# Two clears of unused rows, moved among the block loads of a batch, in a fused Fourier mixing and SwiGLU kernel

## The chip, the cores and the metric

The kernel runs on one core of a Trainium2 chip. The metric is the device time of one execution in microseconds; lower is better. The core's engines run side by side, each with its own instructions in a fixed order: TensorE (PE in the profile, PEld for its weight loads), VectorE (DVE), ScalarE (ACT), GpSimd (POOL) and SyncE (SP), which here only issues DMAs. Engines wait for each other, and for DMAs, by semaphores. The DMAs of SP stand in one queue (q1 in the profile) and are carried by 16 DMA engines.

## The reference

```
X = np.fft.fft(x, axis=1)            # x: 8 batches, 3008 rows, 256 columns
X = np.fft.fft(X, axis=2)
x = X.real.reshape(24064, 256)
g = x @ w_gate                       # 256 -> 1536
silu = g * (1.0 / (1.0 + np.exp(-g)))
val = x @ w_val
out = (silu * val) @ w_out           # 1536 -> 256
```

## The kernel before

The real part of a two-dimensional Fourier transform has symmetries, and the kernel folds the input by them before it multiplies: rows that differ by a quarter, a half or a reflection of the batch are added and subtracted first, so that the products with the cosine and sine tables are a fraction of the full ones. The transform along the columns is folded into the weights (Wp, Wq, Wm). Each column of the folded problem yields two output rows, a "plus" and a "minus" one.

**Stages.** Batch 0 is loaded and transformed by a prologue written out by hand. All the rest is a stream of units: 24 tiles of up to 512 columns, 12 slices of the hidden width each. A unit does its gate and value products (L1105 on PE), its activations (ACT), its products of gate and value (DVE, or POOL at L1213 and L1256), and the output products (L1283 on PE) follow one tile later. Between the units the later batches are loaded (SP), folded (POOL, the lines L214 to L238) and transformed (L1414 on PE).

**What sets the order.** A planner (class Sched) is given every operation with an estimated time, its dependencies and a due time, chooses the order on each engine, and then issues all operations in that order. So each engine's order is fixed when the program is built. The planner decides by its own estimates, not by what an operation really issues: an operation that issues two DMAs is one entry to it.

**A batch's input.** It goes into two buffers, XA and XC (128 rows of 16 x 256 floats each). XA takes the 128 fold positions from one side, XC the other 60 positions. A batch uses 64 of XC's 128 rows: the second batch (b = 1) rows 64 to 127, a later even batch rows 0 to 63. Each half has 60 rows of data and 4 unused ones, 60 to 63 and 124 to 127. `load_c` returns the steps that fill one half:

- 15 rising blocks (L197), each 4 rows by 4 x 512 floats, 32 KB
- 4 falls (L199), each 60 rows by 512 floats, 120 KB
- a single row (L201), 4 x 256 floats, 4 KB: the batch's first row, which goes into row 124 (60 for even batches), the first of the four unused rows

The unused rows take part in the fold and the products and must hold zeros. `clear_rest` (L326) writes them with one DMA a half, 4 rows by 16 x 256 floats, 64 KB, from a row of zeros kept in Af, a scratch buffer of the fold that POOL clears at L611. The clears are needed once: no later load but the single row writes these rows. The single row lies in a row that a clear writes, so it must come behind the clear of its half.

`load_a` fills XA in the same way: 16 rising blocks of 8 rows (L188, 64 KB each) and 4 falls of 128 rows (L190, 256 KB each). For the second batch XA's rising blocks overwrite space in which the raw weights lay, and its falls space in which the angles of the odd tables lay.

**SP's order around the change.** It is: the loads of batch 0; the 15 rising blocks of XC, the 4 falls, the two clears and the single row; 14 rising blocks of XA; L1569, which copies the first row of a tile's Qt to 16 rows (br); the last two rising blocks; L1577, which spreads br to 128 rows (bc) and waits for br to land; the 4 falls of XA; and then the next loads, the stores of finished output (L1295) and so on. SP's DMAs use eight completion semaphores in turn, and each DMA waits for the one that used its semaphore before, which was issued eight places earlier.

**What the loads feed.** The fold of XC on POOL (L214 to L238, two halves q = 0 and 1, ten instructions each) reads all rising blocks and falls of XC and the clear of its half; the single row is read by the second half alone. Then POOL folds XA in the same ten steps (on 128 rows). Among these steps stand POOL's products of gate and value, L1256, each of which reads a pair of slices from one of two buffers, sv0q and sv1q. ScalarE (L1225) and VectorE (L1249) write the next pair into the same buffer when L1256 has read it.

In the unit loop, the diff touches the place where the steps of the second batch's XC are put on the list of loads:

```
        if i == 1:
            steps = load_c(1, nc.sync)
            pad_row = steps.pop()
            steps.append(lambda: [clear_rest(...) for h in range(2)] + [pad_row()])
            loads.extend((("C", 1), k, fn) for k, fn in enumerate(steps))
```

Of the kernel before, what the change touches and what calls it, by code (L numbers as in the profile page):

```python
# [71 lines left out]
def kernel(  # L72
# [33 lines left out]
    NCR = GH - P  # L106

    def width(t):
        return wide[t]
# [76 lines left out]
    def load_a(b, q):  # L186
        X3 = XA.rearrange("p a q d -> p a (q d)")
        return ([lambda h=h: q.dma_start(out=X3[LA * h:LA * (h + 1), 0:4, :],  # L188
                                         in_=up_block(b, JA - LA * h, LA)) for h in range(NA)] +
                [lambda a=a: q.dma_start(out=X3[:, 4 + a, :], in_=down_set(b, a, JA, LA, NA)) for a in range(4)])  # L190

    def load_c(b, q):

        X3 = XC.rearrange("p a q d -> p a (q d)")
        p0 = 64 * (b % 2)
        pm = p0 + NCR
        return ([lambda h=h: q.dma_start(out=X3[p0 + LC * h:p0 + LC * (h + 1), 0:4, :],  # L197
                                         in_=up_block(b, JC - LC * h, LC)) for h in range(NC_)] +
                [lambda a=a: q.dma_start(out=X3[p0:p0 + NCR, 4 + a, :], in_=down_set(b, a, JC, LC, NC_))  # L199
                 for a in range(4)] +  # L200
                [lambda: q.dma_start(out=XC[pm:pm + 1, 0:4, 1],  # L201
                                     in_=rows_at(b, 0, [[R * D, 1], [R * D, 4], [1, D]]))])
# [121 lines left out]
    def clear_rest(hi, zeros, r0):  # L324
        n = zeros.shape[0]
        nc.sync.dma_start(out=X3c[64 * hi + NCR + r0:64 * hi + NCR + r0 + n, :].rearrange("p (c d) -> p c d", d=D),  # L326
                    in_=zeros.unsqueeze(1).to_broadcast([n, 16, D]))
# [282 lines left out]
    zeros = Af.rearrange("p a b d -> p (a b d)")[:, 0:D]  # L610
# [16 lines left out]
    def pq_tiles(t):  # L627
        if t not in ptile:
            w = width(t) + B if t == nT - 1 else T
            ptile[t] = (pqp if t < nT - 1 else const).tile([P, w], BF16, name="Pt")  # L630
            qtile[t] = (pqp if t < nT - 1 else const).tile([P, w], BF16, name="Qt")
        return ptile[t], qtile[t]
# [155 lines left out]
    def rows(r0, n, step):  # L788
        return out[r0:r0 + step * (n - 1) + 1:step, :]
# [297 lines left out]
    def pe_us(n):  # L1087
        return (n + 6) / 2400

    def act_us(n, ptr=0, sbuf=0):  # L1090
        return n / 1200 + (0.088 if sbuf else 0.0605) + 0.1245 * ptr
# [17 lines left out]
    def bank(k):  # L1109
        return PS[:, (0, 7, 6, 3, 2, 5, 1, 4)[S.place[k[0]]], :]  # L1110
# [20 lines left out]
    def turn(unit, step):  # L1131
        S.turn = (*unit.u, step == "b")
        getattr(unit, step)()
        S.turn = None
# [207 lines left out]
    def run_loads(n):  # L1342
        for what, k, fn in loads[:n]:
            up = NA if what[0] == "A" else NC_
            k_ = k if what[0] == "A" else k % (NC_ + 5)
            S.add("SP", 0.35 if k_ < up else 0.62 if what[0] == "A" else 0.9, fn, w=[((what[0],), k)], lat=LOAD_LAT,
                  ring=RING.get(what, RING[what[0]])[k_ >= up],
                  after=[(("A",), "pre" if k >= NA else "preW")] if what == ("A", 1) else ())
        del loads[:n]
# [222 lines left out]
    def all_rows(t):  # L1572
        w = row_width(t)

        def fn():
            bc[t] = bcp.tile([P, T], BF16, name="bc")
            nc.sync.dma_start(out=bc[t][:, :w], in_=T_["br", t][0:P:8, :w].unsqueeze(1).to_broadcast([16, 8, w]))  # L1577
        return fn
# [13 lines left out]
    for i, u in enumerate(units):  # L1592
        t, f = u
        for op in before.pop(i, ()):
            op()
        if i == 1:
            steps = load_c(1, nc.sync)
            pad_row = steps.pop()
            steps.append(lambda: [clear_rest(1 - h, zeros[64 * (1 - h) + NCR:64 * (1 - h) + 64], 0) for h in range(2)] + [pad_row()])
            loads.extend((("C", 1), k, fn) for k, fn in enumerate(steps))  # L1600
        if i == 8:
            loads[0:0] = [(("A", 1), k, fn) for k, fn in enumerate(load_a(1, nc.sync))]
        run_loads(LOADS)
        if i == FIRST - 1:
            kb = (("B", "bc", 3), 0)

            def first_copy():
                bc[3] = bcp.tile([P, T], BF16, name="bc")
                nc.scalar.copy(bc[3][:, :width(3)], bank(kb)[:, :width(3)])

            S.add("PE", pe_us(T), lambda: nc.tensor.matmul(bank(kb)[:, :width(3)], sel, pq_tiles(3)[1][:, :width(3)], start=True, stop=True),
                  r=[(("pq", 3), "Q")], w=[kb], new=[kb[0]], cat="pe", bits=(0, width(3)))
            S.add("ACT", act_us(T), first_copy, r=[kb], w=[(("bc", 3), 0)], new=[("bc", 3)])
        for j, k in enumerate((i - ROW_GAP, i)[::-1]):
            tr, fr = divmod(k, nF)
            if k >= 0 and fr == {0: 11, 1: 3, 2: 99}.get(tr, 6) and tr + 1 < nT:
                if j:
                    S.add("SP", 0.55, all_rows(tr + 1), r=[(("br", tr + 1), 0)], w=[(("bc", tr + 1), 0)], new=[("bc", tr + 1)], lat=5.0, ring=0.4)
                else:
                    S.add("SP", 0.55, first_rows16(tr + 1), r=[(("pq", tr + 1), "Q")], w=[(("br", tr + 1), 0)], new=[("br", tr + 1)], lat=4.0, ring=0.2)  # L1620
        if i == 2 * nF + 1:
            S.add("ACT", 1.36, lambda: nc.scalar.activation(Wm[:, 1], Wm[:, 1], AF.Copy, scale=-0.5),
                  r=[(("Wm",), (fc, 1)) for fc in range(1, 3)], w=[(("Wm",), 1)])
        if i == nF + 1:
            S.add("DVE", 0.5, lambda: vts(Wg[:, 0], Wm[:, 0], scalar1=-0.5, scalar2=None, op0=Alu.mult),
                  r=[(("Wm",), (fc, 0)) for fc in range(1, 3)], w=[(("Wg",), 0)])
        turn(U[i], "a")
        if owork:
            owork.run(4)
        if i + 1 < len(units):  # L1630
            turn(U[i + 1], "seed")
        if prev is not None:
            turn(U[i - 1], "b")
            if prev[1] == nF - 1:
                owork = OWork(prev[0])
            if owork:
                owork.run(4)
        for what, j in fold_at.get(i, ()):
            fold_step(what, j, i)
        for what in act_at.pop(i, ()):  # L1640
            load_next(what)
        if i in spread_at:
            spread_op(spread_at[i])
        if i in job_at:
            transform_op(*job_at[i])
        prev = u
# [36 lines left out]
```

## Time and profile before

| | |
|---|---|
| median of 3 runs | 606.92 us (605.4 to 607.07) |
| the profiled execution | 604.51 us |
| its span, from the first to the last instruction | 602.7 us |
| granted TensorE clock, mean | 1.00 |
| PE busy | 594.7 us, 99% of the span |
| ACT, DVE, POOL busy | 567.2, 561.3, 547.0 us |
| read from HBM, written to it | 29.43 MB, 24.65 MB |

The profile is a page on one execution and a trace that can be asked for more. Views used below:

- the stretches: busy time of each engine in a window of time, in the order PE, PEld, DVE, ACT, POOL, each with its count of instructions in brackets, then the granted clock, the mean busy share of the 16 DMA engines and the GB/s that they moved
- the timeline: start and duration in us, engine, line, operation, what it writes and reads, shapes, count, and in square brackets the idle time of the engine before it with what ended it; instructions of a kind that follow each other are one row, and SPq is SP's issuing of DMAs, not their transport
- the waits: who waited for whom, in us in total, how often, and the longest
- the list of DMA issues: target and source, count, KB each and, where it is known, us from issue to landing

Idle time of an engine that is not the bottleneck costs nothing by itself.

### The profile page before, as it was taken

What the parts mean: (1) busy time and instruction counts of PE and PEld (TensorE: products, weight loads), DVE (VectorE), ACT (ScalarE), POOL (GpSimd) and SP (SyncE); (2) the same over time, 40 slices, a digit from 0 to 9 for tenths busy, and PEclk for the clock granted to TensorE, in tenths of its full rate; (3) what the DMA queues carried; (4) which work ended last, traced back from release to release, by engine and by line L of the source; (5) the groups of instructions that cost most, each with busy time, mean ns of one, the idle gap of its engine ahead of it and who ended that gap; (6) DMA issues with size and microseconds to landing.
All of it is one profiled execution on the core that took longest, in us unless ns stands there. A gap on an engine that the chain in (4) does not pass through costs nothing.

```text
span 602.7 us, 12697 instructions
## 1 busy us (share of the span) xinstructions
PE 594.7 (99%) x4050; PEld 393.1 (65%) x4050; DVE 561.3 (93%) x1044; ACT 567.2 (94%) x1100; POOL 547.0 (91%) x508
## 2 busy tenths in 40 slices
PE   8999989999999999999999999999999999999997
PEld 6545657666666766666666666666666666666686
DVE  8768989989889999999999999999999999999994
ACT  7899889999998999999999999999999899999995
POOL 7978899999999999999998999998989889868873
PEclk9999999999999999999999999999999999999999
DMA  9835437445504514454223412236121211212112
GB/s 242 134 85 127 135 110 188 122 116 133 145 21 112 152 55 130 119 137 129 62 68 96 111 45 63 72 82 174 47 62 36 66 44 46 61 47 68 53 54 79
DMA packets 49968, 57.70 MB, mean 96 GB/s; under 512 B 7256, under 2 KB 36956, under 8 KB 49902
## 3 DMA queue, kind: packets, MB, share of 16 engines
q1 hardware_dynamic: 46947, 53.64, 33.2%
q0 software_dynamic: 2448, 2.36, 2.6%
q10 hardware_dynamic: 507, 0.91, 0.6%
q8 instruction: 31, 0.51, 0.3%
q14 instruction: 35, 0.29, 0.2%
HBM read 29.43 MB, written 24.65 MB: 90 GB/s over the span
## 4 chain that ended last, share of the span: by engine, by line
PE 90%; ACT 4%; POOL 2%; DMA 1%; issue 1%; DVE 1%; POOLq 0%; ACTq 0%; DVEq 0%
PE ps L1105 44%; PE ps L1283 40%; PE ps L1414 4%; DMA XA<-in_x_dram 1%; PE ps L654 1%; POOL hm L1256 1%; DVE SA L503 0%; PE ps L494 0%; PE ps L545 0%; ACT Tab L429 0%; PE ps L528 0%; ACT wk5s L1225 0%; ACT Tab L1552 0%; ACT SDf L423 0%; ACT wk0s L1193 0%
## 5 line engine op out<-in xcount | busy, mean ns | idle before, releaser
L1105 PE MATMUL ps<-Pt,Wp 128*128 128x512 bf16 (+2 forms) x576 | 203.1, 375 | 0.9 <-ACT sv0q L1225 0.3
L1283 PE MATMUL ps<-Wo,hm 128*128 128x256 bf16 (+2 forms) x1140 | 164.3, 273 | 0.0
L1283 PE MATMUL ps<-Wo,hp 128*128 128x256 bf16 (+2 forms) x1140 | 162.7, 272 | 0.0
L1105 PE MATMUL ps<-Qt,Wq 128*128 128x512 bf16 (+2 forms) x440 | 159.9, 375 | 0.0
L1283 PEld LDWEIGHTS <-hm 128*128 128x128 bf16 (+2 forms) x1140 | 111.8, 98 | 58.1 <-issue 1.1
L1283 PEld LDWEIGHTS <-hp 128*128 128x128 bf16 (+2 forms) x1140 | 112.0, 98 | 53.0 <-issue 0.3
L1256 POOL TENSOR_TENSOR hm<-sv0q 128x1024 bf16<-128x1024 f32 (+2 forms) x68 | 126.7, 1864 | 9.9 <-ACT sv0q L1225 5.6
L1256 POOL TENSOR_TENSOR hm<-sv1q 128x1024 bf16<-128x1024 f32 (+2 forms) x66 | 122.9, 1863 | 9.0 <-DVE sv1q L1249 3.9
L1105 PE MATMUL ps<-Qt,Wm 128*128 128x512 bf16 (+2 forms) x286 | 102.1, 376 | 2.2 <-ACT wk2s L1193 1.6
L1168 ACT ACTIVATE ps<-bc,w 128x512 f32<-128x512 bf16 (+2 forms) x136 | 95.7, 718 | 0.5
L1105 PEld LDWEIGHTS <-Wp 128*128 128x128 bf16 x576 | 56.2, 98 | 31.1 <-issue 3.5
L1225 ACT ACTIVATE sv0q<-ps 128x512 f32<-128x512 f32 (+1 forms) x87 | 57.5, 672 | 3.0 <-PE ps L1105 1.4
L1105 PEld LDWEIGHTS <-Wq 128*128 128x128 bf16 x440 | 43.0, 98 | 26.5 <-issue 2.4
L1225 ACT ACTIVATE sv1q<-ps 128x512 f32<-128x512 f32 (+1 forms) x85 | 55.6, 668 | 3.8 <-POOL hm L1256 3.0
L1105 PEld LDWEIGHTS <-Wm 128*128 128x128 bf16 x286 | 27.9, 98 | 15.7 <-issue 1.3
L214 POOL TENSOR_TENSOR SDf<-XA 128x1020 f32<-128x1020 f32 x14 | 33.0, 2360 | 4.5 <-DMA out_dram<-wk7s 4.5
L224 POOL TENSOR_TENSOR Af<-EOf 128x516 f32<-128x516 f32 (+1 forms) x22 | 24.2, 1102 | 0.4
L221 POOL TENSOR_TENSOR EOf<-SDf 128x512 f32<-128x512 f32 (+1 forms) x22 | 24.0, 1093 | 0.0
L218 POOL TENSOR_TENSOR EOf<-SDf 128x512 f32<-128x512 f32 (+1 forms) x22 | 24.0, 1092 | 0.0
L1178 DVE SCALAR_TENSOR_TENSOR wk10s<-bc,w,ps 128x512 f32<-128x512 bf16 (+2 forms) x32 | 23.2, 726 | 0.2 <-PE ps L1105 0.2
L1105 PE MATMUL ps<-Qt,Wg 128*128 128x512 bf16 (+2 forms) x61 | 22.6, 371 | 0.0
L1414 PE MATMUL ps<-Tab,St 128*128 128x376 bf16 (+1 forms) x64 | 20.0, 323 | 0.0
(447 smaller groups left out, 1411.5 us busy)
## 6 DMA issues: line engine op xcount, KB each, us to landing
XA<-in_x_dram SPq DMA_DIRECT2D x30, 256.0 KB
XA<-in_x_dram SPq DMA_DIRECT2D x112, 64.0 KB
XC<-in_x_dram SPq DMA_DIRECT2D x31, 120.0 KB
XC<-in_x_dram SPq DMA_DIRECT2D x105, 32.0 KB
bc<-br SPq DMA_DIRECT2D x21, 128.0 KB
out_dram<-wk0s SPq DMA_DIRECT2D x19, 128.0 KB
St<-Fc SPq DMA_DIRECT2D x14, 128.5 KB
out_dram<-wk7s SPq DMA_DIRECT2D x13, 128.0 KB
```

Of the source, the lines that this page charges most:

```text
L214: tt(F[:, :, 1:D], up[:, :, 1:D], down[:, :, D - 1:0:-1], op=Alu.add)
L218: tt(E[:, :, 0:P], F[:, :, P:0:-1], F[:, :, P:D], op=Alu.add)
L221: tt(O[:, :, 0:P], F[:, :, P:0:-1], F[:, :, P:D], op=Alu.subtract)
L224: tt(Af[r], EOf[r, :, 0:2, :], EOf[r, :, 2:4, :], op=Alu.add)
L654: nc.tensor.matmul(ps[:, e], Z0[:, q, k, :], Tab[:, c, q, 0, e], start=False, stop=True, skip_group_check=True)
L1105: nc.tensor.matmul(ps[:, :n], Wt[:, gv, fs], src[:, :n], start=start, stop=stop, skip_group_check=True)
L1168: nc.scalar.activation(bank(k)[:, :self.wp], bc[self.t][:, :self.wp], AF.Copy, scale=w0[:, gv, self.f:self.f + 1])
L1178: nc.vector.scalar_tensor_tensor(work(e)[:, :self.wp], bc[self.t][:, :self.wp], w0[:, gv, self.f:self.f + 1], bank(k)[:, :self.wp], op0=Al ...
L1225: return lambda: nc.scalar.activation(self.silu(self.sm, w), src()[:, :w], AF.Silu)
L1256: lambda: nc.gpsimd.tensor_tensor(tiles_of(t)[1][:, f - 1:f + 1, :w], pair(self.vm)[:, :, :w, 1], pair(self.vm)[:, :, :w, 0], op=Alu.mult),
L1283: nc.tensor.matmul(bank(ko)[:n, j * D:(j + 1) * D], hts[t][minus][:, f, c:c + n], Wo[:, f, :], start=(f == 0), stop=(f == nF - 1))
L1414: nc.tensor.matmul(ps[:, cols], l, r_, start=(i == 0), stop=(i == len(mms) - 1), skip_group_check=True)
```

## The change

The two clears are no longer issued in one step with the single row behind the falls. The clear of rows 124 to 127 is issued in the same step as the ninth rising block of XC, right behind it, and the clear of rows 60 to 63 with the tenth. The single row is a step of its own behind the falls. The list of loads is as long as before (20 steps), and the planner's entries keep their times and dependencies, so that its order of entries is the same on every engine.

```
@@ -1596,7 +1596,13 @@
         if i == 1:
             steps = load_c(1, nc.sync)
             pad_row = steps.pop()
-            steps.append(lambda: [clear_rest(1 - h, zeros[64 * (1 - h) + NCR:64 * (1 - h) + 64], 0) for h in range(2)] + [pad_row()])
+            for h in range(2):
+                def clear_too(rows=steps[8 + h], hi=1 - h):
+                    rows()
+                    clear_rest(hi, zeros[64 * hi + NCR:64 * hi + 64], 0)
+
+                steps[8 + h] = clear_too
+            steps.append(pad_row)
             loads.extend((("C", 1), k, fn) for k, fn in enumerate(steps))
```

In SP's queue the second batch's XC then reads: 9 rising blocks, a clear, a rising block, a clear, 5 rising blocks, 4 falls, the single row.

## The prediction

> **What bounds the kernel now.** I read the page first, then the busy time by stretches, then the waits of TensorE, and from the largest one back through the engines that it hangs on. In the rows of part 1 of the page and of the stretches, the figures are busy microseconds.
>
> ```profile
> span 602.7 us, 12697 instructions
> PE 594.7 (99%) x4050; PEld 393.1 (65%) x4050; DVE 561.3 (93%) x1044; ACT 567.2 (94%) x1100; POOL 547.0 (91%) x508
> ...
> 40.00:76.90 36.90, 36.84 (x230) 22.60 (x229) 31.27 (x53) 30.99 (x58) 31.88 (x37) 1.00 0.51 121
> 76.90:81.00 4.10, 2.24 (x13) 1.11 (x12) 3.72 (x6) 3.85 (x8) 4.02 (x4) 1.00 0.33 100
> 81.00:596.00 515.00, 514.96 (x3541) 345.18 (x3540) 495.81 (x899) 496.47 (x972) 478.67 (x401) 1.00 0.33 88
> ```
>
> PE (first figure after the length) is full from 81 us to the end at a granted clock of 1.00, and full from 40 to 76.9. So a microsecond won before 81 us is kept to the end, and the only PE time to be won behind the start lies between 76.9 and 81. It is made of two waits:
>
> ```profile
> 78.58 0.38 PE L1105 MATMUL ps<-Qt,Wm 128*128 128x512 bf16 x1 [1.60 <-ACT wk2s L1193]
> 80.52 0.38 PE L1105 MATMUL ps<-Pt,Wp 128*128 128x512 bf16 x1 [0.27 <-ACT sv0q L1225]
> ...
> 76.93 0.64 ACT L1225 ACTIVATE sv1q<-ps 128x512 f32<-128x512 f32 x1 [1.81 <-POOL hm L1256]
> ...
> 76.93 0.69 DVE L1249 SCALAR_TENSOR_TENSOR sv1q<-wk4s,ps 128x512 f32<-128x512 f32 x1 [1.65 <-POOL hm L1256]
> ```
>
> PE waits for ScalarE, and ScalarE and VectorE both stand until POOL's product L1256 has freed the buffer sv1q. Together 1.60 + 0.27 = 1.87 us, 0.31% of the time: this is the most that the change can bring, since a bound behind POOL would only lower it.
>
> POOL does that product late because its fold of the second batch (L214 and on) stands in front of it, in order:
>
> ```profile
> 62.25 2.35 POOL L214 TENSOR_TENSOR SDf<-XA 128x1020 f32<-128x1020 f32 x1 [4.51 <-DMA out_dram<-wk7s]
> ...
> 64.72 1.90 POOL L1256 TENSOR_TENSOR hm<-sv0q 128x1024 bf16<-128x1024 f32 x1
> ...
> 72.52 2.36 POOL L214 TENSOR_TENSOR SDf<-XA 128x1020 f32<-128x1020 f32 x1
> ...
> 74.98 1.91 POOL L1256 TENSOR_TENSOR hm<-sv1q 128x1024 bf16<-128x1024 f32 x1
> ```
>
> From 62.25 to 76.89 POOL has no gap: no row between them shows one. Before 62.25 it idles 4.51 us. The releaser is named after a store, whose completion counter the loads share; L214 reads XA, and what it needs is the last load of XA. SP's queue shows why that load is late:
>
> ```profile
> 21.70 8.78 SPq L197 DMA_DIRECT2D XC<-in_x_dram  x15
> 30.84 3.53 SPq L199 DMA_DIRECT2D XC<-in_x_dram  x4
> 34.62 2.16 SPq L326 DMA_DIRECT2D XC<-Af  x2
> 40.29 0.65 SPq L201 DMA_DIRECT2D XC<-in_x_dram  x1
> 41.17 7.14 SPq L188 DMA_DIRECT2D XA<-in_x_dram  x14
> 48.86 0.59 SPq L1569 DMA_DIRECT2D br<-Qt  x1
> 49.57 1.02 SPq L188 DMA_DIRECT2D XA<-in_x_dram  x2
> 54.35 0.61 SPq L1577 DMA_DIRECT2D bc<-br  x1
> 55.06 2.51 SPq L190 DMA_DIRECT2D XA<-in_x_dram  x4
> ...
> SPq L201 <- DMA XC<-Af: 3.4, 1, 3.4
> SPq L1577 <- DMA br<-Qt: 3.7, 1, 3.7
> ```
>
> The single row (L201) waits 3.4 us for the clears (L326) to land, and all behind it waits too: the sixteen rises of XA (L188), the row copies L1569 and L1577, the four falls of XA (L190), and then POOL. How the transfers fill the DMA engines meanwhile (the last two figures are the mean share of 16 engines and GB/s):
>
> ```profile
> 33.00:37.00 4.00, 3.81 (x38) 1.74 (x37) 2.55 (x6) 4.00 (x8) 2.64 (x6) 1.00 0.54 125
> 38.50:41.00 2.50, 2.50 (x17) 1.56 (x16) 2.12 (x5) 2.45 (x6) 2.27 (x6) 1.00 0.19 31
> 41.00:42.00 1.00, 1.00 (x7) 0.49 (x5) 1.00 (x2) 1.00 (x2) 1.00 (x1) 1.00 0.03 9
> 42.00:43.00 1.00, 1.00 (x8) 0.58 (x6) 0.49 (x2) 1.00 (x4) 1.00 (x1) 1.00 0.43 125
> 43.00:53.00 10.00, 10.00 (x55) 5.12 (x53) 8.35 (x17) 9.10 (x18) 9.84 (x14) 1.00 0.54 87
> ```
>
> The clears run alone on 0.19 x 16 = 3 engines until 41, then almost nothing moves for 1 us, and from 42 on XA's rises keep 0.54 x 16 = 8.6 engines full for ten microseconds.
>
> **The change part by part.** No instruction of PE, DVE, ACT or POOL is added, taken away or moved. SP issues the same 22 DMAs for XC; the two clears now stand behind the ninth and tenth rise instead of behind the falls. So two clears are passed by the last five rises and the four falls, the tenth rise by one, and the wait of L201 for a clear becomes a wait of the clears' followers for a place in flight: SP keeps eight DMAs in flight, each new one waiting for the one issued eight before (so the built program has it). The clears themselves gain no wait of substance: what they need of POOL (the zeroed rows, and the last reader of the space they overwrite) ends before 23 us, ahead of the ninth rise:
>
> ```profile
> 15.38 0.32 POOL L611 MEMSET Af<- 128x256 f32 x1
> 21.78 1.13 POOL L406 TENSOR_SCALAR XA<-XC,cols 128x376 int32<-128x376 f32 x2
> 26.29 0.25 SPq L197 DMA_DIRECT2D XC<-in_x_dram  x1
> 30.23 0.25 SPq L197 DMA_DIRECT2D XC<-in_x_dram  x1
> ```
>
> *What SP's order gives.* The last two rows are the ninth and the fifteenth rise: 6 steps in 3.94 us, 0.66 us each. Eight in flight make 5.3 us, so the ninth rise lands near 26.3 + 5.3 = 31.6. A clear of 64 KB at the 31 GB/s of its row takes 2.1 us. The clear behind it lands at 33.7, the tenth rise at 34.3, the second clear at 36.5. In the new order the third fall waits for the second clear's place: 36.5. Then the fourth fall, L201 and the first rise of XA follow at 0.88 us each (3.53 / 4 for a fall; 41.17 - 40.29 behind L201): 39.1, against 41.17 now. That is 2.0 us. The upper bound of the clears' cost here: the load of Wo shares these engines until 37.3,
>
> ```profile
> Wo<-in_moe_w_out_dram POOLq DMA_DIRECT2D x1, 768.0 KB, 14.4
> 22.86 0.87 POOL L739 DMA_DIRECT2D Wo<-in_moe_w_out_dram  x1
> ```
>
> and if it halves the rate of the first clear (4.2 us in place of 2.1), the rises of XA begin at 41.2: gain nothing.
>
> *What the engines' work gives.* The clears are not made smaller, and their bytes now lie ahead of the falls' on the same few engines. Those engines were busy to 41.0 (their row), so XA's rises can begin there at about 41.1, if the same work takes the same time, against 42.0 now: 0.9 us, the empty microsecond of the row 41 to 42. The Trainium skill, "DMA: Bandwidth & Descriptors", section "Why a DMA increments its semaphore by 16 and not by 1", has a DMA from this queue run on the largest number of engines up to 16 that divides its slowest dimensions, and on the lowest-numbered ones; 4 rows would be the same four engines for rises and clears, 8 rows eight of them. The 3 and 8.6 engines of the rows agree, and by that rule alone the sum would be 0.9 and not 2.0.
>
> Between 0.9 (same work, same engines) and 2.0 (SP's order alone), with 0 at the slow clear, I take 1.0, nearer to the engines' row, since it needs no guess of how two queues share. The bounds kept are -0.5 and 2.0.
>
> *From there to the end.* The rises of XA run at what the row of 43 to 53 allows, 87 GB/s, whenever they begin; L1569 follows the fourteenth of them and waits for nothing else (its source is written at 45.90, below; it is issued at 48.86), L1577 waits for L1569, and the XA falls stand behind L1577. So the fold moves up by the same 1.0. POOL has room: it is idle from 62.25 - 4.51 = 57.74. The product at 64.72 needs sv0q, complete at 62.30, and that at 74.98 needs sv1q, complete at 72.03, so they can move up 2.4 and 2.9 us:
>
> ```profile
> 45.30 0.60 DVE L1439 TENSOR_TENSOR Qt<-ps,wk0s 128x240 bf16<-128x240 f32 x2
> 61.62 0.68 DVE L1249 SCALAR_TENSOR_TENSOR sv0q<-wk9s,ps 128x512 f32<-128x512 f32 x1
> 71.35 0.68 ACT L1225 ACTIVATE sv1q<-wk3s 128x512 f32<-128x512 f32 x1
> ```
>
> 1.0 us off POOL is then 1.0 us off the wait of 1.60.
>
> *What may be late next.* XC's own falls now land behind the clears, near 41.5 in place of 38.5 (from where the clears run alone), and the fold of XC starts at 40.85, right behind other POOL work. A start at 41.5 would cost 0.7 us of the 4.51 us that POOL idles afterwards, so nothing; were that cover gone, 0.7 us.
>
> ```profile
> 40.03 0.73 POOL L1547 MEMSET Tab<- 64x756 bf16 x1
> 40.85 2.35 POOL L214 TENSOR_TENSOR SDf<-XC 64x1020 f32<-64x1020 f32 x1
> ```
>
> Sum: 1.0 us less. The profiled execution took 604.51 us with a span of 602.7; it would take 603.5. It lies 2.4 us under the median of 606.92, and on that scale the change gives 605.9.
>
> **The rivals.** *The whole wait goes.* If the clears run beside the load of Wo at no cost, SP's order decides: 2.0 us, cut to the 1.87 us of the two waits: 605.1. For it: 13 of 16 engines are idle at 38.5 to 41. Against it: the few that carry the clears are not.
>
> *Nothing moves.* The rises of XA begin when their engines are free, and these finish later because falls and clears now meet there: 606.9. For it: 125 GB/s at 33 to 37 with 8.6 engines shows that falls and rises slow each other already. Against it: the empty microsecond at 41 goes in any case.
>
> *The clears hold up the falls.* Place: the queue of eight. The third fall cannot be issued before the second clear has landed, and the fourth, L201 and all of XA stand behind. The tipping point is a landing of the second clear at 38.5 (2.0 us later than in the sum); slower by 0.3% from 40.3 on, that is when both clears take over 8 us in place of 4.2. For it: a clear took 5.6 us from issue to landing (34.62 to the end of L201's wait, 36.78 + 3.4 = 40.2). With 5.6 for the first and 2.1 for the second XA begins 1.5 us later than now: 608.4. With 5.6 for both it is 5 us: 611.9. Against it: most of those 5.6 us were spent behind falls.
>
> **How the numbers follow.** About 0.3% (1.8 us) is what a measurement of this kernel can tell from no change. Forecast (0.5 to 1.6 us less) 0.42; the whole wait 0.23; nothing 0.17; clears late 0.18. Faster by over 0.3%: 0.19 of the whole wait, whose 1.87 us lie just past the bound, and 0.09 of the forecast by scatter: 0.28. Slower: 0.16 of the late clears and 0.03 by scatter: 0.19. The rest, 0.53, is within. The predicted time is 605.9. The range reaches from the whole wait with some scatter, 604.6, to the milder late clear, 608.2; the forecast's own is 605.3 to 606.4.
>
> **What would show it.** In SP's queue L201 no longer waits for XC<-Af, and the first L188 stands near 40 in place of 41.17 (later than 41.17: the clears hold up the falls). In the stretches the row of 41 to 42 is no longer empty. POOL's first fold of XA starts near 61.2 in place of 62.25, and PE's wait of 1.60 us shrinks by as much. The prediction is wrong if the fold of XA moves and PE's wait does not, if L188 moves and the fold does not, or if PE gains a wait before 76 us.

## The result, and the profile after

| | before | after |
|---|---|---|
| median | 606.93 us (605.4 to 607.53, 6 runs) | 602.9 us (602.02 to 604.11, 6 runs) |
| profiled execution, its span | 604.51 us, 602.7 us | 603.96 us, 602.2 us |

The ratio is 0.9937 with a 95% interval of 0.9919 to 0.9956: faster by 4.0 us, and outside the range of the prediction (604.6 to 608.2). The two profiled executions differ by only 0.55 us. So the question of the study is not only what the change does, but where the other 3.5 us are, which this pair of profiles does not show. One execution of the kernel before, among those timed beside the experiments, took 1850.27 us and is left out of all that follows.

What SP does in the changed kernel (timeline: start and duration in us; SPq is the issuing of DMAs):

```profile
21.47 4.62 SPq L197 DMA_DIRECT2D XC<-in_x_dram  x9
26.49 0.79 SPq L326 DMA_DIRECT2D XC<-Af  x1
27.32 0.47 SPq L197 DMA_DIRECT2D XC<-in_x_dram  x1
27.84 0.70 SPq L326 DMA_DIRECT2D XC<-Af  x1
28.58 3.15 SPq L197 DMA_DIRECT2D XC<-in_x_dram  x5
34.17 3.92 SPq L199 DMA_DIRECT2D XC<-in_x_dram  x4
38.14 0.64 SPq L201 DMA_DIRECT2D XC<-in_x_dram  x1
39.03 7.49 SPq L188 DMA_DIRECT2D XA<-in_x_dram  x14
47.14 0.60 SPq L1569 DMA_DIRECT2D br<-Qt  x1
47.95 1.13 SPq L188 DMA_DIRECT2D XA<-in_x_dram  x2
53.51 0.61 SPq L1577 DMA_DIRECT2D bc<-br  x1
54.23 2.51 SPq L190 DMA_DIRECT2D XA<-in_x_dram  x4
```

The single row (L201) goes out right behind the falls; its wait for a clear is gone. Part of that wait now stands ahead of the falls, which wait 2.8 us for the clears: the first fall goes out at 34.17, against 30.84 before. The first rise of XA stands at 39.03, against 41.17 before: 2.14 us earlier. But L1577 is only 0.84 us earlier (53.51 against 54.35). From the first rise to L1577 the changed kernel takes 53.51 - 39.03 = 14.5 us, the kernel before 54.35 - 41.17 = 13.2: most of what SP won is lost again while the rises are carried. The stretches (last two figures: busy share of the 16 DMA engines, GB/s) show the same:

```profile
41.00:42.00 1.00, 1.00 (x7) 0.48 (x6) 0.97 (x2) 1.00 (x3) 1.00 (x1) 1.00 0.51 76
42.00:43.00 1.00, 1.00 (x8) 0.58 (x7) 0.52 (x1) 1.00 (x3) 1.00 (x2) 1.00 0.53 80
43.00:53.00 10.00, 10.00 (x54) 5.08 (x53) 8.25 (x18) 9.10 (x17) 9.84 (x14) 1.00 0.54 77
```

The empty microsecond at 41 is filled, but at the same busy share of 0.54 the ten microseconds from 43 on carry 77 GB/s and not 87. POOL and PE follow (timeline, with the idle time before in brackets):

```profile
40.69 2.35 POOL L214 TENSOR_TENSOR SDf<-XC 64x1020 f32<-64x1020 f32 x1
...
61.63 2.35 POOL L214 TENSOR_TENSOR SDf<-XA 128x1020 f32<-128x1020 f32 x1 [4.07 <-DVE wk1s L1178]
...
77.94 0.38 PE L1105 MATMUL ps<-Qt,Wm 128*128 128x512 bf16 x1 [1.10 <-ACT wk2s L1193]
79.88 0.38 PE L1105 MATMUL ps<-Pt,Wp 128*128 128x512 bf16 x1 [0.26 <-ACT sv0q L1225]
```

The fold of XA begins 0.62 us earlier and PE's first wait shrinks by 0.50. That is the chain that the prediction described, at about half its size, and it accounts for the 0.55 us between the two profiles. The experiments look for the rest.

### The profile page after: what moved, and what is told of

Its sections match the earlier page's. It is cut to its first block, busy times and chain, and to the rows that moved or that the text cites. A ratio compares the mean times of both kernels' runs of the same rounds, so it can differ in the third digit from the quotient of the medians.

```text
span 602.2 us, 12696 instructions
## 1 busy us (share of the span) xinstructions
PE 594.7 (99%) x4050; PEld 393.5 (65%) x4050; DVE 561.0 (93%) x1044; ACT 567.3 (94%) x1100; POOL 546.5 (91%) x508
## 3 DMA queue, kind: packets, MB, share of 16 engines
q0 software_dynamic: 2448, 2.36, 2.6%
## 4 chain that ended last, share of the span: by engine, by line
PE 89%; ACT 4%; DMA 2%; issue 1%; POOL 1%; SPq 1%; DVE 1%; ACTq 0%; DVEq 0%
PE ps L1105 44%; PE ps L1283 39%; PE ps L1414 4%; DMA XA<-in_x_dram 2%; PE ps L654 1%; ACT EOb L556 0%; SPq L197 0%; ACT wk0s L1193 0%; ACT Tab L429 0%; PE ps L528 0%; POOL hm L1256 0%; ACT wk5s L1225 0%; ACT Tab L1552 0%; ACT SDf L423 0%; ACT wk1s L1225 0%
## 5 line engine op out<-in xcount | busy, mean ns | idle before, releaser
L1168 ACT ACTIVATE ps<-bc,w 128x512 f32<-128x512 bf16 (+2 forms) x136 | 95.7, 718 | 0.5
```

The source lines that it names most:

```text
L1168: nc.scalar.activation(bank(k)[:, :self.wp], bc[self.t][:, :self.wp], AF.Copy, scale=w0[:, gv, self.f:self.f + 1])
```

## The experiments

Two theories stood at the start. **Theory A**: everything runs through the late landing of what SP loads behind the clears. **Theory B**: part of the gain lies elsewhere, in the start-up or in the stream behind. After experiment 1 Theory A took its second form: two things hang on XA's rises and not one. Besides the fold, L1569 and L1577 stand among them, and the tile bc that L1577 fills is read by ScalarE at L1168, whose result PE needs for its next product.

**1. Both kernels again.** No edit.

> The kernel before, unchanged, profiled a second time. Theory A: executions differ in how late XA's loads land (the pace of XA's rises differs from one to the next), and PE's wait near 78 us takes that up one for one; the median lies 2.4 us above the profiled execution, so an execution near the median shows a PE wait there of about 1.9 + 2.4 = 4.3 us, with rises of XA about 0.9 us apart in place of 0.78. Theory B: the missing 2 to 3 us lie elsewhere (the start, the tail, or outside the span); then the PE wait stays near 1.9 us whatever the time is.

> The changed kernel, profiled a second time; its timed executions fall into two groups, near 602.05 and near 603.9 us, and the profiled one (603.96) had PE waits of 1.10 + 0.26 us. Theory A: an execution near 602.05 has no PE wait behind 76 us, one near 603.9 has about 1.4 us of it. Theory B: the PE wait is the same in both groups.

The kernel before took 606.24 us this time, and its waits are others than either theory expected: near 78 us there is neither a wait of 4.3 us nor one of 1.9 (timeline):

```profile
42.28 6.99 SPq L188 DMA_DIRECT2D XA<-in_x_dram  x14
...
55.76 0.61 SPq L1577 DMA_DIRECT2D bc<-br  x1
...
59.34 1.30 ACT L1168 ACTIVATE ps<-bc,w 128x512 f32<-128x512 bf16 x2 [2.60 <-DMA bc<-br]
...
60.08 0.59 PE L1105 MATMUL ps<-Pt,Wp 128*128 128x512 bf16 x1 [2.33 <-ACT ps L1168]
63.69 2.36 POOL L214 TENSOR_TENSOR SDf<-XA 128x1020 f32<-128x1020 f32 x1 [5.22 <-DMA XC<-in_x_dram]
```

ScalarE waits for bc, PE waits 2.33 us for ScalarE at 58 to 60 us, and the wait near 78 us is not there: the stop has taken its place. And something follows it (stretches of the same execution; the figure ahead of the last two is the granted clock):

```profile
57.75:60.07 2.32, 0.00 (x0) 0.00 (x0) 0.72 (x2) 0.73 (x2) 0.72 (x2) 1.00 0.78 203
60.07:63.48 3.41, 3.40 (x11) 1.51 (x11) 2.54 (x5) 2.10 (x4) 0.00 (x0) 0.50 0.85 237
```

For 3.41 us behind the stop the clock is 0.50. At half speed that is 1.7 us of work lost. The span of 604.5 us against the shortest of this study, 600.3, is 4.2 us, and 2.33 + 1.7 = 4.0 are nearly as much. (Experiment 5 comes back to this sum: XA's fold was late in this execution too.) The changed kernel took 605.46 us, which is in neither of the two groups expected: its rises began at 39.67, but L1577 stands only at 54.71, and PE waits 1.53 and 0.26 us near 80.

**2. The single row alone, and one clear alone.** `row_late` leaves the clears where the kernel before had them and moves the single row alone; `one_clear_late` is the changed kernel with the clear of rows 60 to 63 put behind XA's last fall.

```
# row_late, against before
-  steps.append(lambda: [clear_rest(...) for h in range(2)] + [pad_row()])
+  steps.append(lambda: [clear_rest(...) for h in range(2)])
...
+  steps = load_a(1, nc.sync)
+
+  def row_too(rows=steps[6], row=pad_row):
+      rows()
+      row()
+
+  steps[6] = row_too
# one_clear_late, against after
-  for h in range(2):
+  for h in range(1):
...
+  def clear_last(rows=steps[19]):
+      rows()
+      clear_rest(0, zeros[NCR:64], 0)
+
+  steps[19] = clear_last
```

> The clears stay behind the falls as before; only the single row is moved, behind the seventh rise of XA, so that XA's first rises are issued without waiting for the clears. If SP's wait alone cost the time, this is as fast as the changed kernel: about 603 us, ratio 0.993 to 0.995. If the clears' place among the rises matters too (they then run beside the load of Wo), XA still begins behind the clears' bytes and it gains half or less: 605 us.

> As the changed kernel, but the clear of rows 60 to 63, which no one needs before the third batch, goes behind XA's falls, so one clear less stands ahead of XA's rises on their engines. Theory A: XA lands some 1.5 us earlier than in the changed kernel, PE's wait behind 76 us is gone in every execution: 602.0 us, all executions alike. Theory B: no difference from the changed kernel, two groups near 602 and 604.

`row_late`: 602.27 us (601.95 to 603.24), ratio to before 0.9942 (0.9922 to 0.9961). Its timeline:

```profile
37.22 4.46 SPq L188 DMA_DIRECT2D XA<-in_x_dram  x7
42.54 0.66 SPq L201 DMA_DIRECT2D XC<-in_x_dram  x1
43.24 4.06 SPq L188 DMA_DIRECT2D XA<-in_x_dram  x7
...
51.40 0.61 SPq L1577 DMA_DIRECT2D bc<-br  x1
...
56.74 1.30 ACT L1168 ACTIVATE ps<-bc,w 128x512 f32<-128x512 bf16 x2
58.90 2.35 POOL L214 TENSOR_TENSOR SDf<-XA 128x1020 f32<-128x1020 f32 x1 [0.94 <-DMA XA<-in_x_dram]
```

```profile
span 600.3 us, 12634 instructions
```

With the clears untouched and only the wait of SP gone, neither PE's stop near 60 nor its wait near 78 is left. This is the floor of the kernel as far as these loads go: 602.0 to 602.3 us, a span of 600.3. It also shows that L1168 begins at 56.74 when nothing holds it. In the first profile of before it stood at 56.90, with no idle time ahead of it: the whole stream was 0.16 us later there (ScalarE's L1193 ahead of it began at 55.31, against 55.15). So bc was not late in that profile, but nearly: L1577 went out at 54.35 there, and in a later profile of before (before_c), at 54.68, bc held up L1168 by 0.41 us.

`one_clear_late`: 603.18 us (602.01 to 607.96). Its slowest run, the profiled one of 607.96 us, has a long wait for a store of output, which SP issues behind the late clear and whose buffer ScalarE needs.

```profile
58.07 0.76 SPq L326 DMA_DIRECT2D XC<-Af  x1
...
68.44 0.60 ACT L1236 ACTIVATE wk7s<-ps 128x512 f32<-128x512 f32 x1 [3.57 <-DMA out_dram<-wk7s]
...
69.09 0.38 PE L1105 MATMUL ps<-Pt,Wp 128*128 128x512 bf16 x1 [2.30 <-ACT wk7s L1236]
```

Its fold of XA is late as well (65.31 us). It met neither expectation and says little about the two theories, beside that a clear placed later is not free.

**3. The two legs one by one.** `xa_late` and `bc_late` are both built on `row_late`. The first issues XA's first six rises once more, behind bc and ahead of the falls: XA late, bc early. The second moves bc behind XA's falls: bc late, XA early. `extra_clear` is the changed kernel with a needless clear ahead of XA's first rise, for the pace of the rises, and `after_b` the changed kernel as it is.

```
# xa_late, against row_late
+  def rises_again(rows=steps[16], again=steps[0:6]):
+      for fn in again:
+          fn()
+      rows()
+
+  steps[16] = rises_again
# bc_late, against row_late: L1577 of tile 1 leaves its place
-  S.add("SP", 0.55, all_rows(tr + 1), ...)
+  S.add("SP", 0.55, all_rows(tr + 1) if tr else lambda: None, ...)
...
+  def bc_behind(rows=steps[19], bc_rows=all_rows(1)):
+      rows()
+      bc_rows()
+
+  steps[19] = bc_behind
# extra_clear, against after
+  def clear_again(rows=steps[0]):
+      clear_rest(0, zeros[NCR:64], 0)
+      rows()
+
+  steps[0] = clear_again
```

> The kernel with the single row behind XA's seventh rise, with one more change: XA's first six rises are issued a second time behind bc and ahead of the four falls, so bc is as early as there and XA's last landing some 4 us later (six times 0.62 to 0.85 us). Theory A: no wait near 58 us, XA's fold near 62.5 to 63.5 us, PE waits at 78 to 80 us by 1.9 to 2.7 us, the clock stays at 1.0: 604.2 to 605.0 us, so the leg over POOL by itself is worth 2 to 2.5 us, and not the 4.0 us between the two kernels. Theory B (the fold alone carries it): 606 us or more with bc early.

> The kernel with the single row behind XA's seventh rise (602.27 us, profiled 602.07), with one more change: the load of bc for the second tile (L1577) is issued behind XA's four falls (L190) and no longer ahead of them. XA's own loads are as early as there, or earlier by the one issue. Theory A in its second form (two things hang on XA's rises: the fold on POOL, and bc, which ACT at L1168 needs at 56 to 57 us): bc lands near 59.3 us, PE stops for 2 to 2.5 us near 58 to 60 us, nothing waits near 78 us, and the granted clock falls to 0.5 for some 3.4 us behind it, as in the second profile of the kernel before; 604.6 us without the fall of the clock, 606.2 us with it. Theory B (the fold on POOL alone carries the change, and bc has slack): XA's fold at 58.9 us or before, no wait of PE, 602.3 us.

> The changed kernel with one needless DMA more: rows 60 to 63 of XC are cleared a second time directly ahead of XA's first rise, where nothing waits for it but the fold of XC. It should tell why XA's rises went at 0.62 us each where the clears were still in the queues, and at 0.78 to 0.91 us where they had drained. Theory A (a DMA that still holds some of the engines puts the engines of the rises out of step, and out of step they move faster): the rises go at 0.62 to 0.70 us each although there is more to move, bc and XA land earlier than in the changed kernel, 602.0 to 602.5 us. Theory B (the pace is that of the memory or of chance): 0.85 us each, all of it 0.6 to 1.5 us later, 603.5 to 606 us.

> The changed kernel unchanged, beside the three others on the same chip. Both theories: 602.0 to 604.1 us as before; it gives the difference to the kernels of this call. Theory A: where bc lands before 56.9 us there is no wait near 58 us and the clock stays at 1.0; the time is then 602.2 us plus the wait near 78 us.

`xa_late`: 604.28 us (603.58 to 606.44), the time that Theory A expected (604.2 to 605.0); the fold and PE's wait moved less than it said (62.5 to 63.5 us, and 1.9 to 2.7 us). The profiled run took 604.24, with bc on time (L1168 at 56.75) and this (timeline):

```profile
61.86 2.35 POOL L214 TENSOR_TENSOR SDf<-XA 128x1020 f32<-128x1020 f32 x1 [4.31 <-DMA out_dram<-wk7s]
...
78.16 0.38 PE L1105 MATMUL ps<-Qt,Wm 128*128 128x512 bf16 x1 [1.33 <-ACT wk2s L1193]
80.09 0.38 PE L1105 MATMUL ps<-Pt,Wp 128*128 128x512 bf16 x1 [0.26 <-ACT sv0q L1225]
```

A fold 3.0 us later than in `row_late` costs a span 2.1 us longer (602.4), of which PE's waits show 1.6. The leg over POOL alone is worth about 2 us.

`bc_late` missed what Theory A expected and gave the time of Theory B: 602.04 us (601.98 to 602.39) and no stop of PE. Its rises went so fast (the next point) that L1577 went out at 49.83 although it stood behind the falls, and bc still landed in time. It took a stronger edit (4). `after_b` gave 602.68 us (601.97 to 606.22), ratio 0.9965 (0.9944 to 0.9987) beside runs of the kernel before with a median of 605.21: on this chip the gain is 2.1 us by the ratio and 2.5 by the medians, and not 4.0. Two of those 26 runs of the kernel before took 602.12 and 602.14 us, so that kernel too is at the floor now and then. `extra_clear` gave 604.52 us (602.63 to 606.07), slower than `after_b` by 1.8, with the pace of Theory A and the time of Theory B: its rises went at the same pace (6), but the third went out at 42.83 us, against 41.00 in `after_b`, behind one clear more.

**4. bc late for certain, and more profiles of before.** In `bc_thrice` the load L1577 of `bc_late` is made three times into the same tile, each behind the landing of the one before.

```
-  nc.sync.dma_start(out=bc[t][:, :w], in_=...)
+  for _ in range(3 if t == 1 else 1):
+      nc.sync.dma_start(out=bc[t][:, :w], in_=...)
```

> The kernel with bc behind XA's four falls (602.04 us; bc landed near 54.8 us there, ahead of its need at 56.0 us, since the rises went at 0.40 us each), with the load of bc (L1577) made three times over into the same tile, each load behind the landing of the one before: bc lands 4 to 5 us later, near 59.3 us, while XA's loads stay as early as they were. Theory A, second form (bc is a second leg, and it has no slack): PE stops for 2 to 3 us near 58 to 60 us, nothing waits near 78 us; 604.3 to 605.1 us if the granted clock stays at 1.0, 606.0 to 606.8 us if it falls to 0.5 for 3.4 us behind the stop. Theory B (a late bc is taken up by slack behind it): 602.0 to 602.5 us with no stop of PE longer than 0.5 us.

> The kernel before unchanged, one more look, since its times on one chip run from 602.12 to 607.15 us and the two profiles of it differ in which wait PE had. Theory A, second form: the time is 602.0 us plus what PE waits for the two legs (bc near 58 to 60 us, XA's fold near 78 to 81 us) plus half of the stretch at the lower clock, to 0.4 us; the pace of XA's rises tells which execution is slow: 0.5 us each gives 602 to 603 us, 0.8 us each 604.5 to 607 us. Theory B: the time differs by more than 1 us from that sum, and what is missing lies in the start-up ahead of 38 us or behind 90 us.

> The same as before_b, a further look, with the same expectations: Theory A, 602.0 us plus PE's two waits plus half of the stretch at the lower clock, to 0.4 us. Theory B, over 1 us away from it.

> The kernel with the single row behind XA's seventh rise and bc behind XA's four falls, once more, for a second profile and more times: its five times so far lay within 601.98 and 602.39 us, with XA's rises at 0.40 us each. Theory A, second form: it depends on the pace. At 0.6 us a rise or less bc lands before 57 us and XA's fold is before 60 us: 602.0 to 602.4 us. At 0.8 us or more bc lands behind 57 us, PE stops near 58 us and the time is 603 us or more. Theory B: 602.0 to 602.4 us at any pace.

`bc_thrice`: 609.6 us (608.85 to 610.02). Its timeline, and a stretch of it:

```profile
51.23 9.15 SPq L1578 DMA_DIRECT2D bc<-br  x3
...
58.31 2.34 POOL L214 TENSOR_TENSOR SDf<-XA 128x1020 f32<-128x1020 f32 x1
62.27 1.30 ACT L1168 ACTIVATE ps<-bc,w 128x512 f32<-128x512 bf16 x2 [5.56 <-DMA bc<-br]
63.02 0.59 PE L1105 MATMUL ps<-Pt,Wp 128*128 128x512 bf16 x1 [5.30 <-ACT ps L1168]
```

```profile
61.55:68.38 6.83, 5.36 (x17) 2.80 (x17) 4.54 (x7) 3.85 (x7) 0.00 (x0) 0.50 0.46 116
```

XA's fold is early (58.31) and still the kernel loses 7.6 us, from 602.0 to 609.6: a stop of 5.30 us, and a clock of 0.50 for 6.83 us, of which 5.36 fall behind the stop and cost half, 2.7. That is 8.0, against 7.6 measured. bc is a leg of its own, with hardly any slack behind it (L1168 began 5.5 us late, and PE stopped for 5.30). bc landed later than meant (62.2 and not 59.3), so the 604.3 to 606.8 us of the expectation were too low. `bc_late_b` gave 602.22 us (602.01 to 605.41), with rises nearly as fast as in its first profile (0.46 us each, and 0.40).

The two executions of the kernel before took 604.65 and 605.25 us. Both are more than the sum that Theory A named: 602.0 and the waits of 1.66 and 1.72 us make 603.7, 1.0 and 1.5 us short. What is missing is not where Theory B puts it, though. If the products of VectorE at L1249 are counted through, the same one begins in before_b 0.02 us later than in `row_late` at 59 us, 2.35 later at 77.5 and 2.36 at 94; in before_c 0.09, 3.27 and 3.28. So all is lost between 59 and 78 us, and behind 94 no more than 0.2 us. In before_c 1.2 us are lost by 66 us already: SP's stores of output are late too, ScalarE (L1236) waits 1.74 us for one, until 65.87 us, and PE waits 0.39 and 0.35 us at 66 and 67. So PE's two long waits are not the whole loss; what sets it is the subject of 5.

**5. A longer wait, and three more profiles.** `waits_longer` is the kernel before with a third clear ahead of the single row, so that SP waits longer where the change removed the wait.

```
-  ... for h in range(2)] + [pad_row()]
+  ... for h in (0, 1, 0)] + [pad_row()]
```

> The kernel before with the clear of rows 124 to 127 issued once more ahead of the single row (L201), so that SP waits for a third clear there and XA's rises, br and bc are all some 3 us later than in the kernel before, the clears else where they were. It takes the removed wait and makes it longer. Theory A, second form: bc lands at 59 to 61 us, PE stops for 2.5 to 5 us near 58 to 61 us, the wait near 78 us is swallowed by that stop, and the clock falls to 0.5 for 3.4 us in most executions: 607 to 610 us. Rival (the wait is worth its own length and no more, through the fold of XA alone): the time of the kernel before and 3 us, with a wait of 4.5 to 5 us near 78 us and no stop near 60 us.

> The kernel before unchanged, one more look. Theory A, second form: where it takes over 606.4 us, PE has stopped for bc near 58 us by 2 us or more, with the clock at 0.5 behind it or with a second stop (a copy on ACT, or XA's fold) behind it; the rises went at 0.75 us each or slower. Rival: the slow executions lose their time in the start-up ahead of 38 us, or behind 90 us, with both legs as in the first profile.

> As before_d, a further look, with the same expectations: over 606.4 us only with a stop of PE for bc near 58 us (Theory A), or with time lost ahead of 38 us or behind 90 us (rival).

> As before_d, a further look, with the same expectations: over 606.4 us only with a stop of PE for bc near 58 us (Theory A), or with time lost ahead of 38 us or behind 90 us (rival).

`waits_longer`: 609.08 us (608.71 to 611.41). Theory A expected 607 to 610 us, and its rival, the median of 606.07 us beside these runs and 3 us more, so the time does not tell them apart. In its profile (611.12 us):

```profile
35.89 6.16 SPq L326 DMA_DIRECT2D XC<-Af  x3
45.96 0.65 SPq L201 DMA_DIRECT2D XC<-in_x_dram  x1
46.83 7.43 SPq L188 DMA_DIRECT2D XA<-in_x_dram  x14
...
61.12 0.61 SPq L1577 DMA_DIRECT2D bc<-br  x1
...
64.30 0.58 PE L1105 MATMUL ps<-Pt,Wp 128*128 128x512 bf16 x1 [5.03 <-ACT ps L1168]
...
69.07 2.36 POOL L214 TENSOR_TENSOR SDf<-XA 128x1020 f32<-128x1020 f32 x1 [6.14 <-DMA br<-Qt]
```

No wait is left near 78, and the clock falls as in `bc_thrice` (stretch):

```profile
62.11:68.94 6.83, 4.64 (x15) 2.37 (x15) 4.07 (x6) 3.14 (x6) 0.82 (x3) 0.50 0.86 209
```

The profiles of the kernel before, with all others of the two kernels, are in the table (us; the columns are starts, but for the two of PE's waits, the clock and the last two). "Late" is a product of VectorE at L1249, always the same one, against its start in `row_late` (94.21 us), where nothing waits. Examples of the lines from which its columns are taken, two of before_e and, last, one of `row_late`:

```profile
64.80 2.36 POOL L214 TENSOR_TENSOR SDf<-XA 128x1020 f32<-128x1020 f32 x1 [5.41 <-DMA out_dram<-wk7s]
...
99.10 0.68 DVE L1249 SCALAR_TENSOR_TENSOR sv0q<-wk5s,ps 128x512 f32<-128x512 f32 x1
...
94.21 0.68 DVE L1249 SCALAR_TENSOR_TENSOR sv0q<-wk5s,ps 128x512 f32<-128x512 f32 x1
```

| profile | first L188 | L1577 | L1168 | PE's stop near 60 | PE's waits, 78 to 84 | clock at 0.5 | XA's fold | late | time |
|---|---|---|---|---|---|---|---|---|---|
| before | 41.17 | 54.35 | 56.90 | - | 1.60 + 0.27 | - | 62.25 | 2.35 | 604.51 |
| again_before | 42.28 | 55.76 | 59.34 | 2.33 | - | 3.41 | 63.69 | 3.98 | 606.24 |
| before_b | 40.90 | 53.99 | 56.76 | - | 1.40 + 0.26 | - | 62.29 | 2.36 | 604.65 |
| before_c | 41.03 | 54.68 | 57.12 | - | 1.46 + 0.26 | - | 63.20 | 3.27 | 605.25 |
| before_d | 42.43 | 56.08 | 59.27 | 2.04 | 0.83 + 0.26 | - | 63.64 | 3.74 | 605.94 |
| before_e | 43.17 | 56.85 | 59.45 | 2.20 | 0.21 + 0.26 | 3.41 | 64.80 | 4.89 | 606.94 |
| before_f | 41.51 | 53.47 | 56.76 | - | 1.50 + 0.27 | - | 62.03 | 2.11 | 604.08 |
| after | 39.03 | 53.51 | 56.77 | - | 1.10 + 0.26 | - | 61.63 | 1.71 | 603.96 |
| again_after | 39.67 | 54.71 | 57.17 | - | 1.53 + 0.26 | - | 62.84 | 2.94 | 605.46 |
| after_b | 40.32 | 51.56 | 56.74 | - | - | - | 58.83 | 0.01 | 602.11 |

It is one scale, and XA's fold reads it. In eight of the nine late profiles the fold's start less the lateness is 59.90 to 59.93 us: every microsecond by which the fold starts behind 59.9 is lost, and nothing more. The same holds in `xa_late` (61.86, 1.93 late), `extra_clear` (61.61, 1.70), `one_clear_late` (65.31, 5.38) and `waits_longer` (69.07, 9.16). So PE's stop for bc, the fall of the clock and the wait for a store do not come on top: they lie ahead of the place where POOL's late fold holds up the stream, and take up waiting that would else stand near 78 us. Only in again_before was the stream later by itself (3.98 us) than the fold would have made it (3.8). In `waits_longer`, too, it is the rival's leg over the fold that sets the time, although Theory A's stop near 60 us is there. Nor is it the stop that makes the fold late: the fold began 7.3 to 8.6 us behind L1577 in all ten, 7.6 to 8.0 in the three with a stop.

The change puts the first rise 2.1 us earlier on average (39.67 against 41.78), L1577 1.8 us (53.26 against 55.03) and the fold 2.0 us (61.10 against 63.13). In 16 of 71 timed runs of the kernel before, taken beside the experiments, the mean clock was 0.996 or 0.997, as in the two profiles with a fall, and all 16 took over 606.4 us; in none of 16 timed runs of the changed kernel was it under 0.999.

Not caught: 13 further timed runs of the kernel before over 606.4 us, up to 607.98, with a mean clock of 0.999 or 1.0. No profile of that kernel took more than 606.94 us, so that a still later fold makes these is likely and was not seen.

**6. The pace of the rises.** `both_moved` is the changed kernel with the row moved too, `row_late_b` is `row_late` again, on the same chip.

```
# both_moved, against after
-  steps.append(pad_row)
+  steps.append(lambda: None)
...
+  steps[6] = row_too        # as in row_late
```

> The changed kernel, clears early, with the single row moved behind XA's seventh rise as well: nothing of the clears is in the queues when XA's rises begin, near 38 us. Theory A (a transfer that still holds some of the engines as the rises begin spreads the engines, and spread they are faster): the rises go at 0.64 to 0.90 us each as in the changed kernel, PE waits 0.5 to 1.5 us near 78 us in most executions, 602.3 to 604 us. Theory B (it is the row's place among the rises that makes them faster, or the chip): 0.40 to 0.62 us each and 602.0 to 602.3 us.

> The kernel before with the single row alone moved, once more, on the chip of both_moved. Theory A: the rises go at 0.40 to 0.62 us each, XA's fold begins before 60 us, 602.0 to 602.5 us, and it is not slower than both_moved. Theory B: the same pace as both_moved, whichever that is.

Both reach the floor: 602.21 us (601.97 to 602.39) and 602.21 us (601.95 to 602.76). For `both_moved` that is the time of Theory B at the pace of Theory A, so neither came as written. The pace, taken from the issue times of the ninth to the fourteenth rise, was 0.68 us each in `both_moved` and 0.47 in `row_late_b`. Over the study it was 0.66 to 0.81 in the seven profiles of before, 0.85, 0.90 and 0.64 in the changed kernel, and 0.40 to 0.62 in `row_late`, `row_late_b`, `bc_late`, `bc_late_b` and `xa_late`, where the clears were still being carried as the rises began; in `waits_longer` it was 0.86 and in `one_clear_late` 0.91. `xa_late` issues six rises a second time, from 49.88 us, when the clears are long carried (stretches; share of the DMA engines and GB/s last):

```profile
44.00:46.00 2.00, 2.00 (x15) 1.26 (x13) 1.74 (x6) 1.26 (x3) 1.92 (x3) 1.00 0.49 124
50.00:52.00 2.00, 2.00 (x11) 0.85 (x9) 1.53 (x3) 1.97 (x4) 2.00 (x3) 1.00 0.55 127
52.00:54.00 2.00, 1.93 (x12) 0.99 (x11) 1.34 (x3) 1.98 (x5) 1.92 (x3) 1.00 0.64 87
```

124 GB/s from half of the engines the first time; the second time 127, and then 87 from more of them. But bc, issued at 49.23, and XA's falls, issued from 52.20, share these later rows with the rises, so they do not decide for Theory A's idea that engines which finish out of step get in each other's way less. And `extra_clear` (0.66) and `after_b` (0.64) had the same pace with and without a clear in front. So the cause of the pace stays open; that it differs between executions of one kernel (0.66 to 0.81, 0.64 to 0.90) is shown.

## Why the prediction was wrong

- **"This is the most that the change can bring" (1.87 us): the step that failed.** The leg was the right one, its price was not. It was read from PE's two waits in one execution, and that execution was one of the fast ones. In it the stream is 2.35 us late by 94 us, as the fold at 62.25 gives against 59.9; of the 0.5 us that the waits do not show, 0.16 are lost by 59 us already; where the rest stand is not shown. In the other six profiles of before the fold begins at 62.03 to 64.80 and costs 2.1 to 4.9 us. So what there was to win was 2.1 to 4.9 us, and the change moved the fold by 2.0 us on average and not by the 1.0 of the sum.
- **L1577 was listed among what is late behind the clears, and only the fold was followed from there.** The prediction asked who waits for XA and not who waits for bc. `bc_thrice` shows that a late bc alone can cost 7.6 us. In three of seven profiles of before bc stops PE for 2.0 to 2.3 us, and in two of them the clock falls; but the fold was late by more, or within 0.2 us of as much, so this gap cost the forecast little.
- **"It lies 2.4 us under the median ..., and on that scale the change gives 605.9": wrong for the same reason as the bound.** The 2.4 us were taken as an offset that stays. In the profiles the slower executions are those in which the same loads are later still, and the change moves these loads: 602.9 us, 3.0 under the forecast. For the timed runs that were not profiled this is inferred.
- **What SP's order gives (2.0 us, first L188 at 39.1): right.** Measured 2.14 us and 39.03. The prediction then took 1.0, nearer to the 0.9 of the engines' work, and that choice was wrong for the start of the rises.
- **"The rises of XA run at ... 87 GB/s, whenever they begin": wrong.** It was 77 GB/s in the profiled execution, and between 0.40 and 0.90 us a rise over the study. Because of that the fold moved 0.62 us between the two first profiles, and not the 2.1 us of L188.
- **The leg over POOL: right, and more so than the prediction made of it.** 0.62 us at the fold gave 0.50 at PE's first wait and 0.64 in the stream, no wait came in before 76 us, and `xa_late` shows the whole leg by itself, about 2 us.
- **What may be late next, and the clears that hold up the falls: they did hold them up, and it cost nothing.** The falls waited 2.8 us for the clears (L199 on XC<-Af) and were issued by 38.1, against 34.4 before. XC's first fold began at 40.69, 41.53 and 41.84 in the three profiles of the changed kernel (40.85 in the first of before), and the execution with 41.84 is the one at the floor.
- **What would show it: four of five signs came, nearly as written** (L201 without a wait, L188 at 39.03 where 40 was named, the filled microsecond, PE's wait less by 0.50 where the fold moved by 0.62), and the fold at 61.63 in place of 61.2. They were the right signs, but taken from one execution of each kernel, where they amount to 0.55 us.

## A version that beats both

It is enough to move the one row that waits; where the clears stand then matters little. With the single row moved alone the kernel took 602.27 and 602.21 us, with bc behind the falls besides it 602.04 and 602.22, with clears and row moved 602.21: all at the floor, where the changed kernel took 602.9 and 602.68 us with runs up to 606.22. Of the timed runs with the row moved in these ways 5 of 31 took over 602.5 us, of the changed kernel 8 of 16. Against the kernel before the gain is clear (row alone: ratio 0.9942, 0.9922 to 0.9961); against the changed kernel it is 0.5 us or so, and the intervals of the two ratios overlap. Why the changed kernel, in which the row's wait is gone too, is more often late stays open: in its first profile the rises begin when they do in `both_moved` (39.03 and 39.01) and then go more slowly (0.85 us each against 0.68).

## What to carry to other kernels

When a wait at the head of a queue is removed, list every transfer behind it and the slack of each one's reader, also of the small ones. Where two late legs reach the same stream they do not add, the later one counts: so price a leg by its start against its start in an execution that does not wait (here 59.9 us for the fold), and not by the waits at its end, in which the others may hide. Where the profiled execution is faster than every timed run, the difference need not be an offset: here it was the same loads, later still. So a second profile is worth taking before a gain is bounded. And the cheapest way past a wait is often to move the one instruction that waits, not what it waits for.

## What the runs showed of the hardware

- A stop of PE of 2.20 or 2.33 us was followed by 3.41 us at a clock of 0.50, one of 2.04 (before_d) or of 2.30 us (one_clear_late) was not, and stops of 5.03 and 5.30 us gave 6.83 us. The Trainium skill, "TensorE: Matmul & The Clock Gate", section "What's actually happening", has a free-running window of 3413 ns and half the clock after an idle one. The lengths agree (3.41 and 2 x 3.41 us). Here a stop of 2.20 us, shorter than that window, was enough, and one of 2.30 us was not.
- The same 64 KB loads, at the same busy share of the DMA engines, went at 0.40 to 0.90 us each: from 44 to 48 us again_after has a share of 0.52 and 70 GB/s, `bc_late` 0.52 and 136. A busy share of DMA engines is therefore no measure of what they could still carry.
- In the three executions in which L1577 went out at 55.76, 56.08 and 56.85 us, L1168, waiting for bc, began at 59.34, 59.27 and 59.45: 3.6, 3.2 and 2.6 us behind the issue, against 2.4 in before_c. What held bc in the first two was not looked for.
